# The last projection of a fused convolution and channel-mix kernel: the last four tiles behind the tail, with a PSUM tile and a store each

## The chip, the cores and the metric

The kernel runs on one core of one Trainium2 chip. The metric is the device time of one execution in microseconds (us). A profiled execution gives a second number, its span, from the first to the last instruction in the trace; the execution's own time is a little longer than its span.

## What is computed

Eight sequences of 4160 tokens with 192 channels go through two layers. The first is a causal convolution along the tokens with 7 taps, one set of softmaxed taps for each of 8 heads of 24 channels. The second is a channel mix:

```python
x_prev = x shifted by one token
xk = mu_k * x + (1 - mu_k) * x_prev
xr = mu_r * x + (1 - mu_r) * x_prev
k = max(xk @ w_k, 0)            # 192 -> 1024
v = (k * k) @ w_v               # 1024 -> 192
out = sigmoid(xr @ w_r) * v
```

Inputs and output are float32; the kernel computes in bfloat16 and accumulates in float32.

## The kernel before, in words

Two sequences make a pair, and the four pairs are worked one after the other. The tokens of a pair are cut into steps: of 512 tokens, for the first pair with a half step at both ends, and at the end of each pair a tail of the 64 tokens that are left. A step holds both sequences, so a step of 512 has eight tiles of 128 tokens, and a tail is one tile of 2 x 64.

A step needs three products on TensorE (PE). The K product makes 1024 hidden channels; ScalarE (ACT) applies the relu out of PSUM (line 457) and VectorE (DVE) squares (line 476). The R product (`r`, lines 519 to 522) makes four tiles of tokens at a time, two matmuls each, and ACT applies the sigmoid into `r_sb`. The V product (`v`, lines 526 and 527) takes four tiles of tokens at a time, a *quad*, eight matmuls each (line 505), into one PSUM tile of two banks. Then `v_out` (lines 529 to 544) multiplies all 768 columns by `r_sb` in one DVE operation (line 532) and writes them with one store on SyncE's (SP's) queue (line 541). A tail has versions of its own: `r_tail` and `v_tail` (lines 546 to 561), with one tile of 192 columns, one multiplication (line 557), and a store for each sequence (line 559). At the last pair's tail the second of these goes out on ACT's queue.

All PSUM tiles come from one ring of four (`ring`, two banks each, line 51), which is handed out in program order. A new tile waits until the fourth tile before it has been read. `o_sb`, the result of a quad in SBUF, has three buffers, and all four tiles of tokens lie in it side by side.

The order on each engine is written out by hand. The work is divided into numbered bundles of K slots; tables (`early`, `first`, `xt`, `mixes`, `vq`, `vo`, `late`) say which function runs in which bundle, and the loop at the end of the program (lines 688 to 706) runs, for each bundle, the K products, then `vq`, `mixes`, `vo`, `xt` and `late`, in that order. The loop over `quads` (lines 614 to 621) fills in the V and R work. There are bundles 0 to 67 with K work; bundle 67 holds the last tail's K product, the V product of the last but one quad, then R of the last quad and R of the tail. Bundle 68 has no K work and ends the program: V of the last quad (`vq`), its multiplication and store (`vo`), then the tail (`xt`).

So the last entry of `quads` is the last tail, and `quads[-2]` is the last quad: step 35, second half, eight tiles less the four done in bundle 67. Both have bundle 68.

Of the kernel before, what the change touches and what calls it, by code (L numbers as in the profile page):

```python
# [7 lines left out]
FP32 = mybir.dt.float32  # L8
BF16 = mybir.dt.bfloat16
AF = mybir.ActivationFunctionType  # L10
ALU = mybir.AluOpType
# [3 lines left out]
def kernel(  # L15
# [11 lines left out]
    nc = tc.nc  # L27

    B, S, D = x.shape
# [3 lines left out]
    P = 128  # L33
# [6 lines left out]
    BANK = 512  # L40
# [8 lines left out]
    three = ctx.enter_context(tc.tile_pool(name="three", bufs=3))  # L49
    four = ctx.enter_context(tc.tile_pool(name="four", bufs=4))  # L50
    ring = ctx.enter_context(tc.tile_pool(name="ring", bufs=4, space=bass.MemoryType.PSUM))
# [3 lines left out]
    steps = []  # L55
    slots = []
    first_step = {}
    for p in range(NPAIR):
        sizes = [STEP // 2] + [STEP] * (S // STEP - 1) + [STEP // 2] if p == 0 else [STEP] * (S // STEP)
        t0 = 0  # L60
# [418 lines left out]
    quads = []  # L479
    vb = 1  # L480
    for s, (p, t0, L, n0, ns) in enumerate(steps):
        for j in range(L // 256):
            vb = max(vb, last_bundle[s]) + 1
# [6 lines left out]
    r_sbs = {}  # L490
# [12 lines left out]
    def v_mm(o, s, t):  # L503
        for f in range(NF):
            nc.tensor.matmul(  # L505
                out=o,
                lhsT=k2s[s][:, f, t * P : (t + 1) * P],
                rhs=wv[:, f, :],
                start=(f == 0),
                stop=(f == NF - 1),  # L510
            )
# [40 lines left out]
    def v_tail(s):  # L552
# [5 lines left out]
        for i in range(2):  # L558
            (nc.scalar if i == 1 and p == NPAIR - 1 else nc.sync).dma_start(
                out=out[2 * p + i, t0:S, :], in_=o_sb[i * TAIL : (i + 1) * TAIL, :]  # L560
            )


    early, first, xt, mixes, vq, vo, late = ({} for _ in range(7))

    def at(table, b, fn, *a):
        table.setdefault(b, []).append((fn, a))
# [46 lines left out]
    for s, j, vb in quads:  # L614
        if steps[s][2] == TAIL:
            at(xt, vb - 1, r_tail, s)
            at(xt, vb, v_tail, s)
        else:
            at(vq, vb, v, s, j)
            at(vo, vb, v_out, s, j)  # L620
            at(xt, vb - 1, r, s, j)
# [115 lines left out]
```

## Time and profile before

| what | value |
|---|---|
| time, median of 6 runs | 447.82 us (447.3 to 448.69) |
| the profiled execution: own time | 448.48 us |
| the profiled execution: span | 446.7 us |
| DVE busy | 387.9 us (87%) |
| ACT busy | 353.7 us (79%) |
| stores of 384 KB out of `o_sb`, from issue to landing | 3.0 us, median of 62 |
| stores of 48 KB out of `o_tail` on SP's queue | 2.1 us, median of 7 |
| store of 48 KB out of `o_tail` on ACT's queue | 2.9 us, one |

"Busy" is the time in which an engine has an instruction in work. In timeline lines the first number is the start in us from the start of the span, the second the time that the group took; then come engine, line, operation, what is written and read, and how many instructions. SPq and ACTq are the instruction queues of SyncE and ScalarE: a line with DMA_DIRECT2D there is the issue of a transfer, and not the transfer. "To landing" counts from the start of the issue until all of the transfer's bytes are confirmed. Queue q1 of the DMA engines carries the transfers of SP, q10 those of ACT.

### The profile page before, as it was taken

The page shows a single profiled execution, that of the slowest core. Times are in us where ns is not written, and L with a number is a line of the kernel's source. Part 1 is how long each engine was busy: PE and PEld are TensorE (multiplying, and loading weights), DVE is VectorE, ACT ScalarE, POOL GpSimd, SP SyncE. Part 2 cuts the span into 40 slices and gives each one's busy share as a digit, 9 for nine tenths or more (in the row PEclk, how much of TensorE's full clock was granted, in tenths as well). Part 3 has the DMA queues.
Part 4 walks back from the last instruction along what each step waited for, and adds up shares of the span by engine and source line. Part 5 has one row for each costly group of instructions (what it writes and reads, how often), then busy time and mean ns, then how long its engine had stood idle before and what let it go on. Part 6 is the DMA issues. An engine that isn't in the chain of part 4 may idle for free.

```text
span 446.7 us, 9702 instructions
## 1 busy us (share of the span) xinstructions
PE 429.9 (96%) x3874; PEld 304.4 (68%) x3937; DVE 387.9 (87%) x702; ACT 353.7 (79%) x465; POOL 48.2 (11%) x70
## 2 busy tenths in 40 slices
PE   7789999999999999999999999999999999999995
PEld 3465766766866776676676776667677677766685
DVE  5799799889988989889979998889988898999972
ACT  3788888888897787889888788888988778777771
POOL 8650001102020100012020010010200000000000
PEclk9999999999999999999999999999999999999999
DMA  8999859989495693395799493475964562522113
GB/s 85 141 184 159 190 154 155 154 201 193 124 224 163 137 202 84 91 199 134 162 210 165 121 221 114 110 111 167 196 159 116 162 148 84 111 72 70 63 48 115
DMA packets 133183, 63.64 MB, mean 142 GB/s; under 512 B 84722, under 2 KB 132882, under 8 KB 133138
## 3 DMA queue, kind: packets, MB, share of 16 engines
q1 hardware_dynamic: 94834, 48.28, 41.0%
q0 software_dynamic: 38224, 14.68, 28.7%
q8 instruction: 31, 0.51, 0.5%
q14 instruction: 14, 0.11, 0.1%
q10 hardware_dynamic: 80, 0.05, 0.0%
HBM read 29.39 MB, written 36.99 MB: 149 GB/s over the span
## 4 chain that ended last, share of the span: by engine, by line
PE 86%; ACT 3%; DVE 3%; DMA 3%; POOL 2%; issue 2%; DVEq 0%
PE ps_v L505 37%; PE ps_k L416 36%; PE ps_r L500 4%; PE ps_r L501 4%; PE ps_c L250 4%; ACT y L286 2%; DMA wk<-in_moe_w_k_dram 2%; DMA xb<-in_x_dram 1%; DVE k L476 1%; POOL xb L122 1%; ACT r_sb L522 1%; ACT y L289 1%; DVE o_sb L532 1%; PE ps_vt L505 0%; DVE xk L397 0%
## 5 line engine op out<-in xcount | busy, mean ns | idle before, releaser
L457 ACT ACTIVATE k_sb<-ps_k 128x1024 bf16<-128x1024 f32 x260 | 245.9, 1035 | 14.3 <-PE ps_k L416 11.1
L416 PE MATMUL ps_k<-xk,wk 64*128 64x512 bf16 (+3 forms) x994 | 188.0, 373 | 7.6 <-DMA wk<-in_moe_w_k_dram 1.6
L505 PEld LDWEIGHTS <-k 128*128 128x128 bf16 x2048 | 170.9, 98 | 14.9 <-issue 0.7
L505 PE MATMUL ps_v<-wv,k 128*128 128x192 bf16 x2048 | 179.4, 246 | 0.6 <-ACT k_sb L457 0.6
L476 DVE TENSOR_TENSOR k<-k_sb 128x1024 bf16<-128x1024 bf16 x256 | 168.0, 685 | 10.2 <-ACT k_sb L457 9.2
L416 PEld LDWEIGHTS <-wk 64*128 64x128 bf16 (+1 forms) x1056 | 66.4, 96 | 103.4 <-issue 55.8
L532 DVE TENSOR_TENSOR o_sb<-ps_v,r_sb 128x768 f32<-128x768 f32 x64 | 61.1, 955 | 26.7 <-PE ps_v L505 26.3
L522 ACT ACTIVATE r_sb<-ps_r 128x768 bf16<-128x768 f32 x64 | 53.1, 829 | 24.8 <-PE ps_r L501 24.8
L286 ACT CAST y<-ps_c 120x480 bf16<-120x480 f32 (+6 forms) x84 | 38.4, 515 | 32.8 <-PE ps_c L250 32.8
L122 POOL DMA_DIRECT2D xb<-in_x_dram x36 | 32.2, 898 | 168.9 <-PE ps_k L416 95.2
L500 PE MATMUL ps_r<-wr,xr 128*128 128x192 bf16 x256 | 47.4, 246 | 0.2 <-DVE o_sb L532 0.2
L501 PE MATMUL ps_r<-wr,xr 128*128 128x192 bf16 x256 | 47.4, 246 | 0.0
L397 DVE TENSOR_TENSOR xk<-xk,yT 128x1024 bf16<-128x1024 bf16 (+1 forms) x66 | 36.2, 549 | 2.3
L397 DVE TENSOR_TENSOR xr<-xr,yT 128x1024 bf16<-128x1024 bf16 (+1 forms) x66 | 36.2, 549 | 2.3
L250 PE MATMUL ps_c<-xb,toe 128*128 128x480 bf16 (+4 forms) x144 | 31.1, 322 | 1.5 <-DMA xb<-in_x_dram 1.2
L355 DVE TENSOR_TENSOR d<-yT 128x1536 bf16<-128x1536 bf16 (+4 forms) x38 | 31.8, 836 | 0.1
L394 DVE TENSOR_SCALAR xk<-d,mu 128x1024 bf16<-128x1024 bf16 (+1 forms) x66 | 27.6, 419 | 1.2
L501 PEld LDWEIGHTS <-xr 128*128 128x128 bf16 x256 | 25.1, 98 | 3.9 <-issue 0.4
L500 PEld LDWEIGHTS <-xr 128*128 128x128 bf16 x256 | 25.1, 98 | 3.6
L394 DVE TENSOR_SCALAR xr<-d,mu 128x1024 bf16<-128x1024 bf16 (+1 forms) x66 | 27.0, 410 | 0.0
L289 ACT CAST y<-ps_c 120x480 bf16<-120x480 f32 (+6 forms) x45 | 20.3, 501 | 8.0 <-PE ps_c L250 8.0
L250 PEld LDWEIGHTS <-toe 128*128 128x128 bf16 x144 | 12.8, 98 | 3.4 <-issue 1.3
(57 smaller groups left out, 78.8 us busy)
## 6 DMA issues: line engine op xcount, KB each, us to landing
out_dram<-o_sb SPq DMA_DIRECT2D x62, 384.0 KB, 3.0
y_dram<-y SPq DMA_DIRECT2D x10, 900.0 KB, 6.9
xb<-in_x_dram POOLq DMA_DIRECT2D x14, 480.0 KB, 8.6
xb<-in_x_dram POOLq DMA_DIRECT2D x6, 432.0 KB, 7.4
xb<-in_x_dram POOLq DMA_DIRECT2D x10, 192.0 KB, 6.4
y_dram<-y SPq DMA_DIRECT2D x3, 450.0 KB, 4.1
y_dram<-y SPq DMA_DIRECT2D x1, 810.0 KB, 5.6
xb<-in_x_dram POOLq DMA_DIRECT2D x2, 384.0 KB, 7.4
```

Of the source, the lines that this page charges most:

```text
L250: nc.tensor.matmul(out=ps[:, :, :, i * G : (i + 1) * G], lhsT=toe[:, h, :], rhs=xbs[g][:, :nb, :, h * G : (h + 1) * G], start=True, stop=True,
L286: copy(out=yh[:, :, :, c0 : c0 + n], in_=ps[:BLK, :, :, 0:n])
L394: nc.vector.tensor_scalar(out=o, in0=d[:, sl, :L], scalar1=mu[:, i, part : part + 1], scalar2=None, op0=ALU.mult)
L397: nc.vector.tensor_tensor(out=o, in0=o, in1=yT[:, sl, c0 : c0 + L], op=ALU.add)
L416: nc.tensor.matmul(out=ps[:, i, f * L : (f + 1) * L], lhsT=wk[r, 0 if hi else 1, fs], rhs=xk[r, i if hi else 2, :L], start=start and f == ...
L457: nc.scalar.activation(out=k_sb, in_=ps.rearrange("p a b -> p (a b)"), func=AF.Relu)
L476: nc.vector.tensor_tensor(out=o, in0=i, in1=i, op=ALU.mult)
L500: nc.tensor.matmul(out=o, lhsT=hi, rhs=wr[:, 0, :], start=True, stop=False)
L501: nc.tensor.matmul(out=o, lhsT=lo, rhs=wlo, start=False, stop=True)
L505: nc.tensor.matmul(out=o, lhsT=k2s[s][:, f, t * P : (t + 1) * P], rhs=wv[:, f, :], start=(f == 0), stop=(f == NF - 1),)
L522: nc.scalar.activation(out=r_sbs[s, j], in_=ps, func=AF.Sigmoid)
L532: nc.vector.tensor_tensor(out=o_sb.rearrange("p (b t) d -> p b (t d)", b=2), in0=v_ps.pop((s, j)), in1=r_sbs.pop((s, j)), op=ALU.mult,)
```

## The change

The last quad is taken out of the tables `vq` and `vo` and put into `late` of the same bundle, behind the tail. In place of `v` and `v_out` it runs a new function, `v_last`. This takes a PSUM tile from the ring for each of the four tiles of tokens, with eight matmuls, one multiplication of 192 columns and one store of 96 KB each. The stores of tiles 0 and 2 go out on SP's queue, those of tiles 1 and 3 on ACT's. The R product of that quad stays where it was, ahead of the tail's.

```diff
+    def v_last(s, j):
+
+        p, t0, L, _, _ = steps[s]
+        r_sb = r_sbs.pop((s, j))
+        o_sb = three.tile([P, 4, D], FP32, tag="o_sb", name="o_sb")
+        for k in range(4):
+            ps = ring.tile([P, 2, BANK], FP32, tag="k", name="ps_v")
+            v_mm(ps[:, 0, 0:D], s, 4 * j + k)
+            nc.vector.tensor_tensor(
+                out=o_sb[:, k, :],
+                in0=ps[:, 0, 0:D],
+                in1=r_sb[:, k // 2, k % 2 * D : (k % 2 + 1) * D],
+                op=ALU.mult,
+            )
+            st, c = divmod((4 * j + k) * P, L)
+            (nc.scalar if k % 2 else nc.sync).dma_start(
+                out=out[2 * p + st, t0 + c : t0 + c + P, :], in_=o_sb[:, k, :]
+            )
...
         if steps[s][2] == TAIL:
             at(xt, vb - 1, r_tail, s)
             at(xt, vb, v_tail, s)
+        elif (s, j) == quads[-2][:2]:
+            at(late, vb, v_last, s, j)
+            at(xt, vb - 1, r, s, j)
         else:
             at(vq, vb, v, s, j)
             at(vo, vb, v_out, s, j)
             at(xt, vb - 1, r, s, j)
```

## The prediction

> **What bounds the kernel now.** I read the page first: the busy shares and the shares of the chain that ended last.
>
> ```profile
> PE 429.9 (96%) x3874; PEld 304.4 (68%) x3937; DVE 387.9 (87%) x702; ACT 353.7 (79%) x465; POOL 48.2 (11%) x70
> ...
> PE 86%; ACT 3%; DVE 3%; DMA 3%; POOL 2%; issue 2%; DVEq 0%
> ```
>
> TensorE bounds the body of the kernel, and the change takes no matmul away: 40 matmuls stand in the last bundle before and after. So nothing is to be had ahead of the last matmul, and the question is what stands behind it. The timeline of the last five microseconds shows that:
>
> ```profile
> 441.25 0.96 DVE L532 TENSOR_TENSOR o_sb<-ps_v,r_sb 128x768 f32<-128x768 f32 x1 [2.56 <-PE ps_v L505]
> 442.13 0.35 DVE L557 TENSOR_TENSOR o_tail<-ps_vt,r_tail 128x192 f32<-128x192 f32 x1
> 442.24 0.37 SPq L541 DMA_DIRECT2D out_dram<-o_sb  x1
> 442.51 0.56 ACTq L559 DMA_DIRECT2D out_dram<-o_tail  x1
> 442.70 0.49 SPq L559 DMA_DIRECT2D out_dram<-o_tail  x1
> ```
>
> In the timeline from 434 us on, the work that these wait for is:
>
> ```profile
> 438.36 2.80 PE L505 MATMUL ps_v<-wv,k 128*128 128x192 bf16 x32
> ...
> 439.10 0.32 ACT L550 ACTIVATE r_tail<-ps_rt 128x192 bf16<-128x192 f32 x1
> 440.92 0.68 PEld L505 LDWEIGHTS <-k2t 128*128 128x128 bf16 x8
> 441.00 0.82 PE L505 MATMUL ps_vt<-wv,k2t 128*128 128x192 bf16 x8
> ```
>
> The last matmul ends at 441.82 and the span at 446.7: 4.9 us of the program have no matmul in them. In them the quad's multiplication of 0.96 us holds the tail's back until 442.13; then three stores, of 384, 48 and 48 KB, are issued within half a microsecond. The windows of that stretch (the last two columns are the DMA engines' busy share and GB/s) say when their bytes moved:
>
> ```profile
> 442.60:443.10 0.50, 0.00 (x0) 0.00 (x0) 0.00 (x0) 0.00 (x0) 0.00 (x0) 1.00 0.00 0
> 443.10:444.30 1.20, 0.00 (x0) 0.00 (x0) 0.00 (x0) 0.00 (x0) 0.00 (x0) 1.00 0.95 300
> 444.30:445.20 0.90, 0.00 (x0) 0.00 (x0) 0.00 (x0) 0.00 (x0) 0.00 (x0) 1.00 0.60 147
> 445.20:445.60 0.40, 0.00 (x0) 0.00 (x0) 0.00 (x0) 0.00 (x0) 0.00 (x0) 1.00 0.00 0
> ```
>
> 2.1 us of transfer, nearly all 384 KB plus the tails, lie on the end. From the DMA view of these lines the stores land 3.0, 2.9 and 2.9 us after their issue: at 445.2, 445.4 (ACT) and 445.6 (SP). From there 1.1 us of closing semaphores lead to 446.7.
>
> **The change, step by step.** All times are those of the profiled execution (span 446.7, own time 448.48, so 1.8 us around it). Its time is 0.66 above the median of the six; I work out a difference and take it from the median.
>
> *Matmuls.* Their order is turned round: eight for the tail from 438.36, then four times eight. Spacing before is (441.00 - 438.36) / 32 = 0.0825 us, so the tail's take 0.66 and the tiles begin at 439.02, 439.68, 440.34 and 441.00. The last group ends at 441.82 as before, if no PSUM tile makes it wait. The ring gives the tail the tile of the last K product (read by ACT until 436.1), tile 0 that of the quad before (DVE reads it 437.73 to 438.69), tile 1 that of R (ACT until 439.20), tile 2 that of the tail's R (439.42), tile 3 that of the tail's V (multiplied from about 439.46 to 439.81). The margins are 0.3, 0.5, 0.9 and 1.2 us: cost nothing. Without this cover, a late reader costs its lateness one for one. The tail's squares end at 436.84, so moving the tail forward costs nothing either.
>
> *Multiplications.* One of 0.96 us goes and four of 192 columns come, in the form of line 557 at 0.35: 1.39 in all, 0.43 more for DVE. The first four of the five (tail and tiles 0 to 2) follow their matmuls at 439.46, 439.9, 440.55 and 441.2 and are hidden behind the next group of matmuls, of 0.66. Only tile 3's counts. It waits for PE alone: 441.82 + 0.05 to 0.09 (the quads' gaps from PE to DVE, 437.69 to 437.73 and 441.16 to 441.25) + 0.35 = 442.24. Before, the tail's ended at 442.48: 0.24 gained. What is queued behind each wait on DVE is only the next multiplication.
>
> *Issues.* Three become six, each waiting for one multiplication. On SP stand the tail's first, tile 0 and tile 2; on ACT the tail's second, tile 1 and tile 3. An issue costs 0.35 to 0.6: 0.37 in the 128-row form of line 541, 0.49 to 0.60 in line 559's, 0.42 and 0.59 for the one-row-per-partition loads at line 666. ACT has no computation behind 439.42, SP nothing but stores, and multiplications on one queue come 1.3 us apart. So only the last issue is on the path, from 442.27.
>
> *Transfer.* A lone 384 KB store shows what is fixed and what grows. The windows round the store issued at 428.54:
>
> ```profile
> 428.54:429.40 0.86, 0.86 (x8) 0.31 (x8) 0.57 (x1) 0.48 (x2) 0.00 (x0) 1.00 0.00 0
> 429.40:430.80 1.40, 1.40 (x12) 0.51 (x7) 0.46 (x1) 1.40 (x2) 0.00 (x0) 1.00 0.86 281
> ```
>
> It lands after 2.6 us (line 541's view of that window), and its bytes run at 328 GB/s in the DMA view: 393 KB make 1.2 us, so 1.4 are fixed. The last store has 98 KB, 0.3 us; with an issue of 0.56 instead of 0.37 that is 1.4 + 0.3 + 0.19 = 1.9, landing 444.17 in place of 445.6. The earlier stores are gone by then: tile 2 is issued at 441.6 and lands near 443.5.
>
> *Closing.* 1.1 us as before. SyncE checks its semaphores one after the other, four of them between 445.6 and 445.8; if the last store's is the last checked, up to 0.18 less.
>
> *Sum.* 442.27 + 1.9 + 1.1 = 445.27, less 0 to 0.18: 1.4 to 1.6 gained, I take **1.5**.
>
> *What the trace does not show.* ACT's queue carries one transfer in the whole trace, the tail's 48 KB, and it took 2.9. In the DMA view of 443.1 to 444.3 only q1 moves bytes; q10 starts behind 444.3, when the 384 KB are through, 1.2 us after its issue ended (SP's big store: 0.5). Either it was held up by the big store, or ACT's queue starts slowly. Bounds: the best is SP's shortest issue (1.7, with the 0.18: gain 1.9); the worst is the whole 2.9, and its 0.9 us window of bytes stretched for twice the size (+0.7): 445.87 + 1.1 = 447.0, a loss of 0.3. I take the lone store's row: q10's start falls just where the big transfer ends, and the tail on SP, issued 0.2 later, took as long.
>
> *Two rules of the Trainium skill against it.* In "DMA: Bandwidth & Descriptors", section "Issuing engines are not separate DMA queues", transfers of all issuing engines run on the same 16 DMA engines, and a second queue saves only the time of initiating. By the rows above that is so here: SP alone would be free at about 442.1, before 442.27, so the second queue is worth nothing. The same page, "Bandwidth", gives about 2.0 us plus size over 436 GB/s for one transfer (on GpSimd's queue) and wants large batches. By it the last store costs 2.2, an estimate, and the gain would be 1.2; it puts 384 KB at 2.9 where the lone store has 2.6. Four small stores cost more in sum, but three of them lie beside matmuls.
>
> **The rivals.**
>
> *A slow queue of ACT.* The 2.9 is ACT's own, not the big store's doing. With 0.15 for the added bytes: 442.27 + 3.05 + 1.1 = 446.4, gain 0.3 to 0.5, **447.4**. For it: the only row. Against it: q10's start at the end of the big transfer.
>
> *One DMA engine late.* The 384 KB store of 438.72 lands after 3.7 instead of 2.6; from 441.0 to 442.1 a DMA share of 0.06, one engine of 16, was still at it, and the view lists an instruction fetch in that stretch. If that hits the last store it costs 1.1: **447.4** also. Against it: the four stores issued between 416 and 435 all landed after 2.6. This is also the way in which the change would not do what it says, which is to take the transfer off the end.
>
> *Slower: the stores gate the multiplications.* All four slices lie in one `o_sb`. If DVE may not write slice k+1 until the store of slice k has landed, each step is 0.03 + 1.9 + 0.05 + 0.35 = 2.3 us: tile 0 ends at 440.25, tile 3 at 447.15, the span at 450.2, **451.3**. One such wait (tile 3 on tile 2, 441.55 + 2.3) gives 446.9, about even; from two on it is slower. Against it: `yT` is written by a transfer while DVE reads other columns of it, without a wait:
>
> ```profile
> 386.18 2.89 SPq L309 DMA_TRANSPOSE yT<-y_dram  x1
> ```
>
> DVE's line 397 reads `yT` at 386.72 and 387.71, with no idle time before it.
>
> **Numbers.** 0.2% (0.9 us, to 446.9) is about what a measurement of this kernel can tell from no change. The forecast's case, 445.9 to 446.7: 0.67, all faster. ACT's slow queue 0.13 and the late engine 0.10, within 0.2%. Gated stores 0.06, slower; 0.04 for any wait of the like that I do not see, slower. So faster 0.67, same 0.23, slower 0.10. The time is 447.82 - 1.5 = **446.3**. The range goes from the best bound (gain 1.9, 445.9, less 0.1) to the two cases at 447.4: 445.8 to 447.5.
>
> **What would show it.** Right: last matmul within 0.1 of 441.8; five short multiplications, the last 0.1 behind PE; ACT's last issue near 442.3; last landing 1.9 later; 1.1 us to the end. Wrong: a landing near 2.9 (ACT's queue), DMA share of 0.06 at the end (a late engine), idle time of DVE before the multiplications of `v_last` ended by a DMA (gated stores), PE idle ahead of a `ps_v` group (the ring).

## The result, and the profile after

The changed kernel takes 446.16 us (median of 23 runs, 445.52 to 447.61) where the kernel before takes 447.49 (median of 47 runs). The ratio is 0.9970, with a 95% interval of 0.9963 to 0.9977: 1.0 to 1.7 us faster. The forecast was 446.3, a gain of 1.5 from a median of 447.82 that the kernel before had then.

The profiled execution of the changed kernel took 446.23 us, with a span of 444.5. That is 2.25 less than the profiled execution of before, but not all of it belongs to the change. The timeline of its last microseconds:

```profile
437.33 0.82 PE L505 MATMUL ps_vt<-wv,k2t 128*128 128x192 bf16 x8
437.37 0.81 ACT L522 ACTIVATE r_sb<-ps_r 128x768 bf16<-128x768 f32 x1 [2.27 <-PE ps_r L501]
437.69 0.37 SPq L541 DMA_DIRECT2D out_dram<-o_sb  x1
437.99 2.80 PE L505 MATMUL ps_v<-wv,k 128*128 128x192 bf16 x32
```

The last matmul ends at 440.79, against 441.82 before. This microsecond was won in work that both kernels share. The profiled executions of the kernels below put this point between 440.7 and 441.7, but for one kernel in which TensorE waits, and the executions of the kernel before alone run from 446.90 to 449.02 us; so I take it for the spread of the executions. What the change can move is the stretch from the last matmul to the end of the span, and I read every kernel by it: **446.67 - 441.82 = 4.85 us before, 444.52 - 440.79 = 3.73 after.** That is 1.12 us less, from one profiled execution of each. The stretch begins so, in the timeline from 440 us on, with the last issue in the timeline from 441 us on:

```profile
440.17 0.36 DVE L571 TENSOR_TENSOR o_sb<-ps_v,r_sb 128x192 f32<-128x192 f32 x1 [0.30 <-PE ps_v L505]
440.83 0.36 DVE L571 TENSOR_TENSOR o_sb<-ps_v,r_sb 128x192 f32<-128x192 f32 x1 [0.30 <-PE ps_v L505]
```

```profile
441.22 0.34 ACTq L578 DMA_DIRECT2D out_dram<-o_sb  x1
```

The multiplications of tiles 1 to 3 now wait for TensorE, each for its own eight matmuls, and the last one ends 0.40 us behind the last matmul (before: 0.66). The DMA issues and landings of the last 9.6 us (line of the store, queue, number, size of one, median us from issue to landing):

```profile
out_dram<-o_sb SPq DMA_DIRECT2D x1, 384.0 KB, 4.6
out_dram<-o_sb SPq DMA_DIRECT2D x2, 96.0 KB, 3.1
out_dram<-o_sb ACTq DMA_DIRECT2D x2, 96.0 KB, 2.7
out_dram<-o_tail SPq DMA_DIRECT2D x1, 48.0 KB, 3.7
out_dram<-o_tail ACTq DMA_DIRECT2D x1, 48.0 KB, 3.9
```

These are long: the big store of the quad ahead takes 4.6 where the four big stores before it take 2.6, and the small stores behind it 2.4 to 3.9. The issues in the queues of SyncE and ScalarE show it too:

```profile
439.40 1.42 SPq L578 DMA_DIRECT2D out_dram<-o_sb  x1
```

```profile
439.90 0.91 ACTq L578 DMA_DIRECT2D out_dram<-o_sb  x1
```

The other two issues of line 578 take 0.40 and 0.34. Something held up the middle of the chain, and the windows of the end say what it looks like (the last two columns are the share of the 16 DMA engines that is busy, and GB/s):

```profile
442.30:442.90 0.60, 0.00 (x0) 0.00 (x0) 0.00 (x0) 0.00 (x0) 0.00 (x0) 1.00 0.48 161
442.90:443.20 0.30, 0.00 (x0) 0.00 (x0) 0.00 (x0) 0.00 (x0) 0.00 (x0) 1.00 0.07 23
443.20:443.40 0.20, 0.00 (x0) 0.00 (x0) 0.00 (x0) 0.00 (x0) 0.00 (x0) 1.00 0.00 0
```

From 442.9 to 443.2 a share of 0.07 fits one engine of 16 (1/16 is 0.06), still at work when the others are done. The last store, issued at 441.22, lands after 2.4 us, at 443.6, and 0.9 later the span ends. In the same trace one instruction fetch, a transfer that brings an engine the next part of its program, stands at 438.7 (queue q8), just when the big store's bytes begin to move. The DMA view from 438.6 to 439.0 us has it:

```profile
q8 instruction: 1, 0.02, 27.4%
```

### The profile page after: what moved, and what is told of

The parts are those of the page before. It is cut to its first block, busy times and chain, and to the rows that moved or that the text cites. A ratio compares the mean times of both kernels' runs of the same rounds, so it can differ in the third digit from the quotient of the medians.

```text
span 444.5 us, 9710 instructions
## 1 busy us (share of the span) xinstructions
PE 430.6 (97%) x3874; PEld 304.7 (69%) x3937; DVE 388.4 (87%) x705; ACT 353.7 (80%) x465; POOL 48.0 (11%) x70
## 4 chain that ended last, share of the span: by engine, by line
PE 88%; DVE 5%; ACT 4%; issue 2%; ACTq 0%
PE ps_v L505 37%; PE ps_k L416 36%; PE ps_r L500 4%; PE ps_r L501 4%; PE ps_c L250 4%; ACT y L286 2%; DVE k L476 2%; PE warm L652 1%; ACT k_sb L457 1%; PE ps_vt L505 1%; ACT y L289 1%; DVE d L355 1%; DVE xk L397 1%; DVE xk L394 1%; ACT r_sb L522 0%
## 5 line engine op out<-in xcount | busy, mean ns | idle before, releaser
L532 DVE TENSOR_TENSOR o_sb<-ps_v,r_sb 128x768 f32<-128x768 f32 x63 | 60.2, 956 | 24.3 <-PE ps_v L505 23.9
```

Source lines behind the costliest of these rows:

```text
L532: nc.vector.tensor_tensor(out=o_sb.rearrange("p (b t) d -> p b (t d)", b=2), in0=v_ps.pop((s, j)), in1=r_sbs.pop((s, j)), op=ALU.mult,)
```

## The experiments

My theory after this: the chain of the forecast is right, and what is missing from its gain is one late DMA engine, kept by TensorE's instruction fetch, on which every store has a share. The rivals: ScalarE's queue, or short stores, are slow of themselves; the order (the tail ahead) is the gain, not the sizes; the second queue is worth nothing. None of these kernels leaves out any of the work. The table gives, for each, the median, its ratio to the kernel before with the 95% interval, and from the profiled execution the stretch in us from the last matmul's end to the end of the span.

| kernel | us | ratio | last matmul to end |
|---|---|---|---|
| before | 447.49 | 1 | 4.85 |
| the change | 446.16 | 0.9970 (0.9963 to 0.9977) | 3.73 |
| order alone | 447.42 | 0.9996 (0.9984 to 1.0007) | 4.73 |
| split, tail last | 446.76 | 0.9975 (0.9965 to 0.9985) | 3.64 |
| one queue | 447.62 | 0.9996 (0.9982 to 1.0011) | 4.78 |
| fetch moved | 445.60 | 0.9946 (0.9933 to 0.9960) | 2.98 |
| fetch less moved | 445.71 | 0.9960 (0.9946 to 0.9973) | 2.98 |
| before, fetch moved | 447.77 | 1.0001 (0.9992 to 1.0010) | 4.87 |
| split, tail last, fetch moved | 446.50 | 0.9974 (0.9964 to 0.9984) | 3.63 |
| one queue, fetch moved | 446.54 | 0.9972 (0.9962 to 0.9982) | 3.88 |
| halves, fetch moved | 446.48 | 0.9979 (0.9970 to 0.9987) | 3.67 |
| one PSUM tile, fetch moved | 447.39 | 0.9995 (0.9986 to 1.0003) | 2.99 |

The kernel before had medians of 447.49 to 447.82 beside these, so the ratio, and not the median, compares kernels. The stretch comes from one execution of each kernel, the ratio from all of its runs.

**Order alone.** The tail first, then the old `v` and `v_out`:

```diff
-            at(late, vb, v_last, s, j)
+            at(late, vb, v, s, j)
+            at(late, vb, v_out, s, j)
```

> The tail goes ahead of the last quad, and the quad stays whole: one PSUM tile, one multiplication of 768 columns, one store of 384 KB. My theory (the gain comes from the size of the last multiplication and store, the order gives none of it): the multiplication ends 1.05 us behind the last matmul, the store lands 2.6 us after its issue, so 4.6 to 4.7 us from the last matmul to the end of the span, against 4.85 before and 3.68 after the change; time 447.3. Rival (the order is the gain, because the small tail no longer queues behind the big store): 3.7 to 4.0 us from the last matmul to the end, time 446.2 to 446.5.

The ratio is 0.9996 and the stretch 4.7: the order by itself gives 0.1. The one big multiplication and store stand behind the last matmul instead of the small ones, and the big store, issued at 441.87, lands after its 2.6. The order is not the gain.

**Split, tail last.** The four tiles keep the quad's place ahead of the tail:

```diff
-            at(late, vb, v_last, s, j)
+            at(vq, vb, v_last, s, j)
```

> The quad is split as in the change, but keeps its place ahead of the tail, which ends the program with a multiplication of 192 columns and a store of 48 KB on each queue. My theory (small last multiplication and store are the gain): the last landing is 2.0 to 2.4 us after the last issue, 3.6 to 3.8 us from the last matmul to the end, time 446.1, the same as the change. Rival (the order is the gain): 4.5 us or more, time 447.0 or more.

Stretch 3.6, ratio 0.9975, as the change: the small last multiplication and stores are the gain, in either order. (That the two orders come out equal has different reasons, as the runs with the fetch moved show below.)

**One queue.** All stores of `v_last` go through `nc.sync`, and those of `v_tail` by the same edit at line 559.

```diff
-            (nc.scalar if k % 2 else nc.sync).dma_start(
+            nc.sync.dma_start(
```

> The change with all stores of tail and quad on SyncE's queue, none on ScalarE's. Theory of one late DMA engine (one of the 16 has been kept by TensorE's instruction fetch at 438.7, and each store has a share on it, so that issues stall and landings wait for it): the issue that took 1.4 us on SyncE in the change now stands ahead of all others; the last issue starts 0.5 to 1 us later, and the time is 446.5 to 447.0. Rival from the forecast (the second queue is worth nothing): 446.2. Second rival (ScalarE's queue is slow of itself): the last landing is 1.9 us after its issue in place of 2.4, time 445.7.

Worse than any theory had it: the whole gain is gone. The timeline of the end shows one stalled issue in front of all others, and four issues that come after it one by one:

```profile
439.56 2.03 SPq L559 DMA_DIRECT2D out_dram<-o_tail  x2
...
441.57 0.36 DVE L571 TENSOR_TENSOR o_sb<-ps_v,r_sb 128x192 f32<-128x192 f32 x1 [0.30 <-PE ps_v L505]
441.68 1.98 SPq L578 DMA_DIRECT2D out_dram<-o_sb  x4
```

The second number of a merged line covers all of the group: the tail's two issues, of 0.49 and 1.48 (line 559's view), reach to 441.6. Tile 0, multiplied since 439.95, is issued only then, and tile 3, whose multiplication ends at 441.93, at 443.26. It lands after 1.7, so the late engine is done by then; the time went into the queue of issues, and 0.4 of it into the closing, which takes 1.4 us here against 0.9 in the change.

**Fetch moved.** TensorE's first warm-up matmuls are cut into four each, which moves every later instruction of its stream by 96:

```diff
-    def warm(n):
+    def warm(n, cols=BANK):
...
-            nc.tensor.matmul(out=ps[:, i % 2, :], lhsT=ones_t, rhs=zeros, start=True, stop=True)
+            nc.tensor.matmul(out=ps[:, i % 2, 0:cols], lhsT=ones_t, rhs=zeros[:, 0:cols], start=True, stop=True)
...
-        warm(WARM)
+        warm(4 * WARM, BANK // 4)
```

> The change, with TensorE's first 16 warm-up matmuls of 512 columns as 64 of 128 columns: the same columns, 96 instructions more, so that TensorE's instruction fetch, which fell at 438.7 us, falls some 4 us earlier. Theory of one late DMA engine: the store of the quad before lands after 2.6 to 3.0 us in place of 4.6, all issues take 0.6 us or less, the last store lands 1.9 us after its issue in place of 2.4, and from the last matmul to the end it is 3.2 us in place of 3.7; time 445.7. Rival (short stores, or ScalarE's queue, take 2.4 us of themselves): 2.4 us, 3.7 us, and 446.2 as the change.

This decides it. The fetch now falls at 436.3, 4.6 us ahead of the last matmul's end in place of 2.1. So queue q8 carries TensorE's instructions: adding some at the start of its stream brought this transfer forward. It meets only the end of the big store before, which lands after 3.2 us, with nothing waiting for it. The DMA view from 436.2 to 436.4 us, and the issues and landings of the last 7 us:

```profile
q8 instruction: 1, 0.02, 30.0%
```

```profile
out_dram<-o_sb SPq DMA_DIRECT2D x1, 384.0 KB, 2.6
out_dram<-o_sb SPq DMA_DIRECT2D x2, 96.0 KB, 1.8
out_dram<-o_sb ACTq DMA_DIRECT2D x2, 96.0 KB, 1.7
out_dram<-o_tail SPq DMA_DIRECT2D x1, 48.0 KB, 1.9
out_dram<-o_tail ACTq DMA_DIRECT2D x1, 48.0 KB, 2.2
```

Every line is shorter than in the change, the same stores in the same order. No issue takes more than 0.6, the last store lands 1.6 us after its issue, and the stretch is 3.0, better than I had expected (3.2). ScalarE's queue is as fast as SyncE's for the 96 KB stores. The 48 KB stores do land 0.3 later on ScalarE's queue than on SyncE's (2.2 against 1.9). This kernel beats both: 445.60, and its interval lies just below the change's (0.9960 against 0.9963).

**Before, fetch moved.** The same edit to the kernel before, as a control.

> The kernel before, with the same 64 short warm-up matmuls in place of 16 long ones, so that its instruction fetch near 439.7 falls some 3 us earlier. Theory of one late DMA engine: in the kernel before the late engine is through at 442.1, and the last stores' bytes start at 443.1, so nothing at the end hangs on the fetch: still 4.8 to 4.9 us from the last matmul to the end, time equal to the kernel before within 0.1%. Rival (the short warm-up matmuls or the place of the fetch speed up the rest of the kernel, and the gain of the experiment that moved the fetch has nothing to do with the last stores): 0.5 us faster than before, as the change gained 0.5 by it.

Ratio 1.0001, stretch 4.9. The short warm-up matmuls give nothing of themselves. The fetch did move, from 439.7 to 435.8, and the late engine went with it: the last big store but one lands after 2.6 us, where it took 3.7, and the share of 0.06 behind it is gone. The windows behind that store, first of the kernel before, then of this one (DMA share and GB/s last):

```profile
441.00:442.10 1.10, 0.82 (x10) 0.59 (x8) 0.85 (x1) 0.00 (x0) 0.00 (x0) 1.00 0.06 18
```

```profile
440.10:441.20 1.10, 0.67 (x9) 0.44 (x6) 1.00 (x2) 0.00 (x0) 0.00 (x0) 1.00 0.00 0
```

In this kernel that is worth nothing, because its last stores move their bytes only when the late engine is through. In these kernels, then, the place of the fetch matters where the last stores follow close behind it.

**Fetch less moved.** The first warm-up matmuls as 48 of 170 columns (`warm(3 * WARM, BANK // 3)`).

> The change, with the first 16 warm-up matmuls as 48 of 170 columns: 64 instructions more in place of 96, so that the fetch falls between its place in the change (2.1 us ahead of the last matmul's end) and that of the run with 96 more (4.6 us ahead). Theory of one late DMA engine: 3.0 to 3.3 us from the last matmul to the end, last landing 1.65 to 1.9 us after its issue, time 445.6 to 445.9. Rival (the gain of the run with 96 more came from the 64 short matmuls themselves, or was chance): 3.6 to 3.7 us, 2.4 us, time 446.2.

The fetch did not fall between the two places: it fell at 435.6, 5.1 us ahead of the last matmul's end, though fewer instructions were added. So it is no test of a middle place, but a second kernel whose fetch is out of the way. The stretch is 3.0 again, the last landing 1.6 behind its issue, ratio 0.9960. By its five runs alone its time is not clear of the change's, since the intervals overlap; the stretch and the landings are what it confirms.

**Split, tail last, fetch moved.**

> The quad split but ahead of the tail, with the fetch moved. The last stores are two of 48 KB in the 64-row form in place of one of 96 KB in the 128-row form. If the order gives nothing and the last store's fixed cost decides: last landing 1.9 to 2.1 us after the issue (the 64-row stores of the run with the fetch moved took 1.9 to 2.2, the 128-row ones 1.6 to 1.9), 3.2 to 3.4 us from the last matmul to the end, time 445.8 to 446.0. If half the size counts: 1.5 us, 2.8, 445.4.

The expectation missed: stretch 3.6, not 3.2 to 3.4, and no gain over the same kernel with the fetch in its old place. There the tail's two stores, issued at 442.22, already landed after 2.0 and 2.2, so the late engine did not reach them. Here they land after 1.9 and 2.2, where the one of 96 KB lands after 1.6. Of the difference of 0.5 on ScalarE's queue 0.2 is the issue (0.54 against 0.34); where the rest lies was not tried apart (64 rows against 128, two stores at once against one). So the order matters after all, once the late engine is gone: 0.65 in the stretch. With the fetch in its old place the change lost 0.75 to the late engine and the other order 0.65 to its last stores, and so the two looked alike.

**One queue, fetch moved.**

> All stores on SyncE's queue, with the fetch moved. Theory (SyncE's queue loses 2 us only because one issue stalls behind the late engine): issues of 0.35 to 0.55 us, none stalls, the last one starts within 0.1 us of the last multiplication's end, 2.9 to 3.1 us from the last matmul to the end, time 445.6, the same as the two queues with the fetch moved. Rival (one queue can't take six stores in 2.5 us, whatever the fetch): the last issue starts 0.5 us or more behind the multiplication, 446.1 or more.

No issue stalls, and still the stretch is 3.9, against 3.0 on two queues. The timeline:

```profile
438.98 1.14 SPq L559 DMA_DIRECT2D out_dram<-o_tail  x2
...
440.21 1.98 SPq L578 DMA_DIRECT2D out_dram<-o_sb  x4
...
440.99 0.36 DVE L571 TENSOR_TENSOR o_sb<-ps_v,r_sb 128x192 f32<-128x192 f32 x1 [0.30 <-PE ps_v L505]
```

The first five issues take SyncE from 438.98 to 441.80, 0.56 each with the gaps between them. So the last starts 0.45 behind the multiplication that it waits for: the rival (0.5 or more) was right but for 0.05. Another 0.4 comes behind the landing: from there to the end it is 1.36 us, against 0.92 on two queues. Why the closing is longer where SyncE issues last stays open.

**Halves, fetch moved.** Two PSUM tiles, multiplications of 384 columns and stores of 192 KB in place of four:

```diff
-        for k in range(4):
+        for h in range(2):
             ps = ring.tile([P, 2, BANK], FP32, tag="k", name="ps_v")
-            v_mm(ps[:, 0, 0:D], s, 4 * j + k)
+            for k in range(2):
+                v_mm(ps[:, 0, k * D : (k + 1) * D], s, 4 * j + 2 * h + k)
...
-            (nc.scalar if k % 2 else nc.sync).dma_start(
+            (nc.scalar if h else nc.sync).dma_start(
```

> The change with the fetch moved, but the quad in two halves: two PSUM tiles, two multiplications of 384 columns, two stores of 192 KB, the last on ScalarE's queue. If the last store and multiplication pay by their size: multiplication 0.55 to 0.6 us in place of 0.36, landing 1.9 to 2.1 in place of 1.65, so 3.4 to 3.6 us from the last matmul to the end, against 2.98 for quarters and 4.7 for the whole quad; time 446.1. If only the number of stores in flight matters, halves do as well as quarters or better: 2.9, 445.5.

The timeline and the landing of the last store:

```profile
440.98 0.56 DVE L572 TENSOR_TENSOR o_sb<-ps_v,r_sb 128x384 f32<-128x384 f32 x1 [0.76 <-PE ps_v L505]
```

```profile
out_dram<-o_sb ACTq DMA_DIRECT2D x1, 192.0 KB, 2.0
```

Size pays as expected, and the stretch, 3.7, is a little above the 3.4 to 3.6 expected. The landings of 1.6, 2.0 and 2.6 us for 96, 192 and 384 KB are about 1.3 plus 0.32 for each 96 KB.

**One PSUM tile, fetch moved.** The quad's tiles share one PSUM tile, as before the change, but are multiplied and stored one by one:

```diff
+        ps = ring.tile([P, 2, BANK], FP32, tag="k", name="ps_v")
         for k in range(4):
-            ps = ring.tile([P, 2, BANK], FP32, tag="k", name="ps_v")
-            v_mm(ps[:, 0, 0:D], s, 4 * j + k)
+            cols = slice(k % 2 * D, (k % 2 + 1) * D)
+            v_mm(ps[:, k // 2, cols], s, 4 * j + k)
```

> The change with the fetch moved, but with the quad's four tiles of tokens in one PSUM tile (two in each bank), multiplied and stored one by one as in the change. If a bank that DVE reads holds up the matmuls that write beside it: TensorE waits some 0.45 us ahead of tile 1 and of tile 3, the last matmul ends 0.9 us later after the R product, time 446.4 to 446.6. If not: time 445.6, as with four PSUM tiles, and the PSUM tile for each tile of tokens is worth nothing.

TensorE waits, and not only where two tiles share a bank. Its timeline:

```profile
438.36 0.82 PE L505 MATMUL ps_v<-wv,k 128*128 128x192 bf16 x8
439.64 0.82 PE L505 MATMUL ps_v<-wv,k 128*128 128x192 bf16 x8 [0.45 <-DVE o_sb L572]
440.90 0.82 PE L505 MATMUL ps_v<-wv,k 128*128 128x192 bf16 x8 [0.45 <-DVE o_sb L572]
442.17 0.82 PE L505 MATMUL ps_v<-wv,k 128*128 128x192 bf16 x8 [0.45 <-DVE o_sb L572]
```

The groups follow each other every 1.27 us in place of 0.66: three waits, one of them ahead of tile 2, which lies in the other bank. So it is the tile and not the bank that is waited for, and the wait is the program's own: in the trace the first matmul of each group waits for the semaphore that DVE's multiplication raises. What the chip would do without that wait was not tried. The last matmul comes 3 x 0.61 = 1.8 us later, and the ratio is 0.9995: without a PSUM tile for each tile of tokens nearly the whole gain of 1.9 us in the stretch is lost again ahead of it.

## Why the prediction was right, and where it was not

**Matmuls and ring: right.** The 40 matmuls take 437.33 to 440.79, 3.46 us, as before. What I did not price is the other side: without four PSUM tiles the waits would have cost 1.8.

**Multiplications: right.** The last one ends 0.40 behind the last matmul; the forecast had 0.42, from the same rows.

**Issues: right that only the last is on the path,** with 0.34 for it where I took 0.56. Two issues stalled (1.42 and 0.91), which I had not foreseen; they did not hold up the last one, which started 0.03 behind its multiplication.

**Transfer: the term that was mis-sized.** The forecast had 1.9 us from the last issue to landing, the change has 2.4, and with the fetch moved it is 1.6. So the fixed part, the bytes and the issue together were 0.3 too dear in the forecast, and the late engine was left out of it. It was there as a rival ("one DMA engine late", 1.1 us, a chance of 0.10), and that rival came true for 0.75 us: 3.73 against 2.98 in the stretch. The chance was too low. The row for it, a landing of 3.7, belonged to the last big store but one, and I weighed it against four undisturbed stores, as if a fetch fell at random. I had also put the fetch into the stretch from 441.0 to 442.1; it stands at 439.7, as that store's bytes begin to move. It falls 2.1 us ahead of the last matmul's end in both kernels, and the change pulls the last stores forward into its reach: the first of them is issued 0.1 us behind it, against 2.5 before. The two errors cancel only in part: 0.5 of the landing is left.

**Closing: right**, 0.93, the lower end of 0.9 to 1.1.

**Sum.** Stretch by the forecast: 4.85 - 1.5 = 3.35, measured 3.73, a gain of 1.12; the ratio's interval, 1.0 to 1.7 us, takes in both gains. That the time came out within 0.14 us of 446.3 is in part luck: a landing 0.5 too long stands against a closing 0.2 shorter, and the kernel before itself measured 0.33 lower in the end (447.49) than the median that I started from. One bound was added up wrongly: the best case, 442.27 + 1.7 + 1.1 - 0.18, is a gain of 1.8, not 1.9.

**The rivals.** ScalarE's queue is not slow for the last store: 1.6 us with the fetch moved, as for the 96 KB store just ahead of it on SyncE's. The 2.9 of its only transfer in the kernel before, where 2.2 is what such a store takes with the fetch moved, fits a wait behind the big store. The stores do not gate the multiplications: in the change tile 0 has no wait, and tiles 1 to 3 wait for TensorE only, 0.30 each.

**The second queue: wrong.** The forecast had SyncE alone free at 442.1, before the last multiplication's end, and so the second queue worth nothing. The five issues ahead of the last need 0.56 each, not some 0.45, and SyncE was 0.45 late even without a stall; with closing that is 0.9 us, and with the fetch in its old place 1.05 of the change's 1.12. The Trainium skill's rule in "DMA: Bandwidth & Descriptors", section "Issuing engines are not separate DMA queues", says that a second queue saves only the time of initiating, usually small beside the transfer. Of the 0.9 us here 0.45 is time of initiating, and the rest a longer closing, of which the section says nothing. That the queues share the engines fits these runs: behind the late engine the tail's stores landed late on both queues (3.7 and 3.9). "Usually small" does not hold at this end, where an issue of 0.34 to 0.59 stands beside 0.3 us of bytes. The same page's fit (it stands under "Anatomy of one DMA — SWDGE (gpsimd) path", and not under "Bandwidth", and is for GpSimd's queue; 2.2 us for this store by the estimate) has 1.6 against it when nothing is in the way.

## What to carry to other kernels

At the end of a kernel count from the last matmul to the end of the span, and make the last multiplication and the last store small: here a store of 96 KB lands 1.0 us sooner than one of 384 KB, and a tile of its own in PSUM lets each part leave while the next is computed. Give the last stores two queues, since issues of half a microsecond in a row are here longer than the 0.3 us of bytes of one store. Then look for single DMA engines that are late (a DMA share near 1/16, landings that are too long all at once), because here every store in flight landed late while one engine was behind (2.4 to 4.6 us, against 1.6 to 2.6).

## What was not expected of the hardware

An instruction fetch of TensorE that starts as a store's bytes begin to move delays the landing of that store and of those behind it, in the change by 0.7 to 2.0 us (4.6 against 2.6 for the big store, 3.7 against 1.9 for the tail's on SyncE, 2.4 against 1.6 for the last), and an issue behind it took 1.42 where 0.54 is what it takes with the fetch moved. It is not only the stores at the end: in the kernel with the fetch moved, the fetch ahead of that one starts at 422.7, 1.05 us behind the issue of a big store, and that store too lands after 4.6 us, where its neighbour issued at 427.64 takes 2.6. A fetch that was over before the bytes moved did no harm: in the kernel before, one stands at 428.2, 0.3 us ahead of the issue of a store, and that store lands after 2.6.

Moving the fetch away from the last stores, by nothing but more instructions in the prologue, gave as much as 0.75 of the 1.87 us between the kernel before and the best one. That the fetch is the cause is shown by moving it, twice, with a control. That what it holds is a single DMA engine, on which every store has a share, is read from the shares of 0.06 and 0.07; and why that engine stays behind so long after a fetch is not shown. Where a fetch falls could not be steered finely: 96 instructions more put it at 436.3, 64 more at 435.6.
